# Gated linear attention and a hard-swish feed-forward on one core: keys and queries turned in token pairs, growth products written over alpha, another order of steps

## The chip, the cores and the metric

One NeuronCore of one Trainium2 chip runs the whole kernel as one launch. The metric is the device time of an execution in microseconds (us). Engines are named as in the profile: PE (TensorE, matmuls), PEld (its weight loads), DVE (VectorE), ACT (ScalarE), POOL (GpSimd) and SP (the queue that issues all DMAs here).

## The reference

Cut to what matters; all tensors are float32 in their values, and the two weight matrices arrive as float64.

```python
# q, k, v, alpha: (B=4, H=8, S=768, D=48)
state = zeros(B, H, D, D)
for t in range(S):
    state = alpha[:, :, t, :, None] * state + einsum('bhd,bhe->bhde', k[:, :, t], v[:, :, t])
    y[:, :, t] = einsum('bhd,bhde->bhe', q[:, :, t], state)
x = y.transpose(0, 2, 1, 3).reshape(3072, 384)
h = x @ w_in                       # (384, 2048)
out = (h * clip(h + 3, 0, 6) / 6) @ w_out   # (2048, 384)
```

## The kernel before, in words

**Chunks.** The recurrence is computed in 24 chunks of 128 tokens, six per batch entry, all eight heads at once as four pairs of heads. A chunk needs keys, queries and alpha with head and feature on the partitions and tokens along the free axis. For chunk j these steps exist, named by the words of the order described below:

- `la`, `lk`, `lq`, `lv`: loads of alpha, keys, queries, values (DMAs on SP, L251 to L272). `ta`, `tk`, `tq`: the turn to feature-major. For chunks 0 to 5 PE does it (L282); from chunk 6 on (`FIRST = 6`) the loads are laid out so that VectorE's 32x32 block transpose does it (L286), writing straight into the tile of the keys or queries, every fourth word in a row. `ca` puts alpha into `aX[j % 2]` (L300 on ScalarE, or L286).
- `r` (`decay`): a scan backwards over alpha gives R (L309), and a reciprocal fills the first column of `ini[j % 2]` (L313). `p` (`growth`): a scan forwards over alpha, started by `ini`, gives P (L320). `k` and `q` (`scaled`): keys times R, queries times P, in place (L332).
- `sc` (L346) is the scores, `m` (L356) the mask, `qa` (L366) places queries for the part of the state, `kb` and `ck` (L374, L378), or `kt`, `kw`, `kr` (a block transpose on VectorE at L391, then out to DRAM and back), bring keys to token-major. `u` (L430) is the update of the state, `sm` (L440) and `st` (L409, POOL) carry the state on, `sv` (L419, ScalarE) puts it beside the values. `ya` and `yb` (L456) are attention over the two halves of the chunk, `cy` (L465) copies the result out as x.

The matmuls of `sc`, `u`, `ya` and `yb` are small: 48x64, 64x48 and 128x32 tiles of the array, 32 records to a step (16 for a `u` with one bank). Everything else on PE uses the whole array. A run of consecutive small steps is called a block below.

**Feed-forward.** Two chunks make a group g of 256 tokens, twelve groups. Groups 0 and 1 multiply by w_in plainly (`f`, `fa`, `fb`: L479, L490). From group 2 on a scheme of 20 products is used: `xc` adds up inputs (VectorE, 128x128), `M` is a product (L603, eight records), `n` (L609, ScalarE) keeps partial sums, `o` (L540 to L544, VectorE) adds up outputs, `e` and `h` (L495 on ScalarE, L499 on VectorE) are the activation. The second matmul is plain for group 0 (`b`, L517); from group 1 on it has seven products `P` (L706, 16 records), with sums `s` (L650, L667), `K` and `G` (copies and sums of outputs) and stores `O`. `w`, `d1` to `d4`, `x`, `y` load and convert the weights early in the run. PE is thus asked for the same matmuls whatever the order.

**The order.** One string of 1798 words, written out in the code, sets the program order of all engines (`with tc.manual_schedule(): run("...")`, from L757 on). A word is a step with its chunk or group and, behind further dots, its part and the PSUM bank that it takes: `sc.9.0.1` is the scores of chunk 9 in banks 0 and 1. Each engine issues its own instructions in this order and waits on semaphores for the others. DMAs stand in the same order on SP's queue. POOL has little in it: conversion of weights early (L217), then `st` and four clears of values (L415).

Of the kernel before, what the change touches and what calls it, by code (L numbers as in the profile page):

```python
# [8 lines left out]
FP = mybir.dt.float32  # L9
# [8 lines left out]
def kernel(  # L18
# [86 lines left out]
    aX, ini = [], []  # L105
    for r in range(2):
        t = consts.tile([C, NP * W + 1], FP, tag=f"ax{r}")
        nc.vector.memset(t, 0.0)
        aX.append(t)
        t = consts.tile([C, NP * W], FP, tag=f"ini{r}")  # L110
        nc.vector.memset(t, 0.0)
        ini.append(t)
# [114 lines left out]
    Ps = consts.tile([C, NP * W], FP, tag="P", name="P")  # L227
# [46 lines left out]
    def transposed(name, j, i=None):  # L274
        if j >= FIRST:
            t = (K_t if name == "k" else Q_t)[j] = (Ks if name == "k" else Qs)[j % 2]
            by_blocks(t, name, j)
            return
        t = bank("t" + name, j, i)
        src = ring[name, j % NR]  # L280
        for p in range(NP):
            nc.tensor.transpose(  # L282
                t[:, p], src[:, 2 * p : 2 * p + 2].rearrange("s h d -> s (h d)"), ident)

    def by_blocks(to, name, j):
        nc.vector.transpose(out=to.rearrange("r p (u v) -> r p v u", v=V),  # L286
                            in_=quads[name, j % NQ][:, :, :, 0:BLK])

# [5 lines left out]
    def without_first(t):  # L294
        return t[:, 0 : NP * W].rearrange("r (p w) -> r p w", w=W)[:, :, 1:W]
# [8 lines left out]
    def decay(j):  # L304

        n = NP * W
        ax, ic = aX[j % 2], ini[j % 2]
# [5 lines left out]
        nc.vector.reciprocal(out=ic.rearrange("r (p w) -> r p w", w=W)[:, :, 0:1],  # L313
                             in_=R_t[j][:, :, 0:1])

    def growth(j):

        n = NP * W
        P_t[j] = Ps
        nc.vector.tensor_tensor_scan(  # L320
            out=P_t[j], data0=aX[j % 2][:, 0:n], data1=ini[j % 2], initial=0.0,
            op0=ALU.mult, op1=ALU.add)

    def scaled(name, j):

        if j < FIRST:
            src = ps_t.pop(("t" + name, j))
            t = (Ks if name == "k" else Qs)[j % 2]
        else:
            src = t = (K_t if name == "k" else Q_t)[j]  # L330
        by = R_t[j][:, :, 1:W] if name == "k" else without_first(P_t.pop(j))
        nc.vector.tensor_tensor(out=t, in0=src, in1=by, op=ALU.mult)  # L332
        (K_t if name == "k" else Q_t)[j] = t
# [423 lines left out]
    with tc.manual_schedule():  # L757
# [14 lines left out]
               d2.8 cy.3 d3.8 fr.0.6.1 w.9 ca.6 w.4 fr.0.7.0 fg.0.7 lv.4.1 ck.4 d2.9 d3.9 f.1.1.1  # L772
               q.4 st.4 d1.9 fr.1.1.0 fg.1.1 sv.4.0 f.1.0.2 ca.5 sc.4.1.0 u.4.1.0 fg.0.6 r.5 d1.4
               f.1.7.0 r.6 f.1.3.3 d4.8 d2.4 w.10 tk.5.3 d4.9 w.11 dx.4 fr.1.7.1 sm.4.0 d3.4 w.12
               d2.10 qa.4.0 fg.1.7 fr.1.3.1 m.4 lq.5 d1.10 f.1.6.0 d3.10 d1.12 d4.4 fr.1.0.0 f.1.2.1
               p.5 fg.1.3 d2.12 k.5 fg.1.0 d3.12 d4.10 fr.1.6.1 sm.4.1 tq.5.1 sv.4.1 lk.6 w.13
               fr.1.2.0 d1.11 f.1.4.2 d2.11 d4.12 fg.1.6 q.5 d3.11 p.6 d2.13 la.7 fr.1.4.1 fg.1.4
               f.1.5.0 lv.5.0 qa.4.1 fg.1.2 kb.5.3 fr.1.5.1 w.15 d4.11 d2.15 ca.7 ya.4.1 qa.5.1 tk.6
               yb.4 sc.5.2.0 b.1.0.2 lk.7 k.6 d3.13 d3.15 st.5 ck.5 fa.4.3 m.5 b.1.1 lq.6 w.14 tq.6
               fb.4 fg.1.5 d1.13 d1.15 d4.15 q.6 b.0.0.1 d2.14 fr.0.4.0 d3.14 y.5 d4.13 cy.4 fg.0.4  # L780
               d1.14 d4.14 x.0 y.1 y.10 b.0.1 y.0 y.2 u.5.2 P.1.0.0 K.1.0 qa.5.0 sv.5.0 qa.6.1
               P.1.1.3 b.0.2 b.1.2 kb.6.0 ya.5.3 y.6 s.1.0.0 sm.5.0 sv.5.1 G.1.0.0 tk.7 s.1.1.1
               s.1.2.3 x.1 yb.5 cy.5 b.1.3 sc.6.1.2 lv.6.2 ck.6 u.6.3.0 s.1.3.2 x.2 P.1.2 b.0.3
               K.1.1 y.7 s.1.4 s.1.5 y.11 y.3 r.7 xc.2.1 x.3 y.4 y.8 xc.2.3 k.7 xc.2.0 xc.2.4 y.9
               y.12 y.16 y.13 y.15 P.1.3.3 K.1.2 P.1.4 bo.1 P.1.5 xc.2.5 G.1.1.1 P.1.6 y.14 y.17
               la.8 xc.2.2 xc.2.6 y.19 G.1.3.3 so.1 y.20 G.1.2.2 y.18 M.2.0.2 bo.0 y.21 M.2.15.3
               y.23 sm.6.0 n.2.0.8 z.1.3 M.2.1 M.2.16 xc.2.8 n.2.1.9 xc.2.7 M.2.2 kb.7.3 p.7 lk.8
               O.1.2 lq.7 xc.2.10 sm.6.1 n.2.2.10 ca.8 m.6 M.2.7.0 lq.8 n.2.7.11 M.2.3 M.2.4 M.2.8
               xc.2.9 lv.7.0 r.8 n.2.4.12 tk.8 ck.7 lv.12.1 k.8 M.2.18.1 sv.6.1 o.2.0.0 st.7 M.2.5
               tq.7 kt.8 kw.8 n.2.5.13 M.2.9 q.7 o.2.1.0 sv.6.0 lq.9 o.2.4.0 u.7.1.3 sc.7.1.3 sm.7.0  # L790
               sv.7.0 O.1.3 M.2.10 ya.6.2 yb.6 e.2.1.1 la.9 h.2.1 e.2.0.0 y.22 lv.8.2 p.8 n.2.10.14
               qa.7.0 M.2.11 sv.7.1 M.2.6.2 n.2.18.10 M.2.19 h.2.0 n.2.11.15 qa.7.1 m.7 O.1.1 M.2.12
               cy.6 o.2.6.0 o.2.5.0 ya.7.1 yb.7 n.2.12.12 kr.8 xc.3.2 y.24 M.2.13 lv.9.0 o.2.3.0
               n.2.13.12 cy.7 tq.8 lq.10 sm.7.1 o.2.3.1 M.2.17 o.2.2.0 e.2.3.0 M.2.14 o.2.2.1 xc.3.1
               xc.3.3 la.10 e.2.2.1 P.2.0.1 xc.3.4 xc.3.5 lk.10 xc.3.6 M.3.0.2 q.8 u.8.1.0 lk.9
               sc.8.2.3 n.3.0.12 M.3.1 h.2.2 e.2.5.1 h.2.3 xc.3.0 xc.3.7 o.2.6.1 e.2.6.0 M.3.7.0
               n.3.1.9 o.2.7.0 o.2.7.1 K.2.0.3 h.2.6 M.3.2 P.2.1 qa.8.0 n.3.7.13 e.2.4.0 n.3.2.10
               xc.3.10 xc.3.8 st.8 h.2.5 ca.9 M.3.3 O.1.0 qa.8.1 h.2.4 r.9 s.2.0.14 G.2.0.1 e.2.7.0
               h.2.7 s.2.1.11 xc.3.9 M.3.4 n.3.4.8 s.2.2.15 M.3.8 P.2.3.3 o.3.0.0 K.2.2 tk.9
               s.2.3.14 s.2.5 k.9 e.3.0.1 M.3.9 o.3.1.0 M.3.5 kt.9 n.3.5.11 P.2.2 sm.8.0 s.2.4 la.11  # L800
               K.2.1 M.3.10 M.3.18.2 P.2.5 sm.8.1 e.3.1.0 n.3.18.15 tq.9 m.8 M.3.19 n.3.10.14 p.9
               M.3.11 ca.10 h.3.0 sv.8.0 q.9 kw.9 qa.6.0 G.2.2.0 kr.9 n.3.11.8 h.3.1 o.3.6.0 sv.8.1
               qa.9.0 P.2.4 o.3.5.0 sc.9.0.1 u.9.2.3 qa.9.1 M.3.12 r.10 n.3.12.10 M.3.15.2 st.9
               tk.10 m.9 M.3.16 M.3.6.3 sv.9.0 G.2.1.2 M.3.13 sm.9.0 o.3.7.0 O.2.2 ya.8.0 yb.8
               o.3.4.0 o.3.3.0 sv.9.1 k.10 ya.9.2 yb.9 n.3.13.10 cy.8 kt.10 sm.9.1 M.3.14 ca.11 cy.9
               o.3.6.1 e.3.5.0 xc.4.1 h.3.5 O.2.1 xc.4.3 xc.4.4 xc.4.0 xc.4.5 e.3.4.1 M.3.17 xc.4.6
               P.2.6 e.3.6.0 st.10 h.3.4 xc.4.2 xc.4.10 lk.11 kw.10 o.3.2.0 o.3.2.1 M.4.0.0 O.2.0
               G.2.3.3 e.3.2.1 xc.4.7 o.3.3.1 o.3.7.1 n.4.0.10 h.3.2 xc.4.8 P.3.0.1 M.4.1 K.3.0.2
               e.3.3.1 h.3.3 n.4.1.13 tq.10 e.3.7.1 P.3.1 p.10 M.4.2 q.10 kr.10 G.3.0.0 lv.10.2
               M.4.7.3 n.4.2.14 la.12 h.3.6 M.4.3 n.4.7.15 h.3.7 lk.12 s.3.0.9 M.4.4 n.4.4.8  # L810
               s.3.1.11 lv.11.0 M.4.8 r.11 P.3.3.2 sc.10.0.2 sv.10.0 s.3.2.12 o.4.0.0 u.10.1.3 tk.11
               O.2.3 M.4.9 s.3.3.9 P.3.2 p.11 K.3.2 k.11 K.3.1 s.3.5 M.4.5 qa.10.0 kt.11 o.4.1.0
               s.3.4 M.4.10 n.4.10.9 m.10 ca.12 P.3.5 sm.10.0 e.4.0.0 lq.11 n.4.5.11 xc.4.9 r.12
               kw.11 M.4.11 G.3.2.1 h.4.0 tq.11 e.4.1.1 la.13 sm.10.1 tk.12 qa.12.0 sv.10.1 M.4.18.0
               P.3.4 n.4.18.12 q.11 kr.11 sv.12.0 M.4.19 G.3.1.3 o.4.6.0 n.4.11.8 M.4.12 o.4.5.0
               st.11 k.12 qa.10.1 u.11.0 lq.12 h.4.1 qa.11.1 sv.11.0 sm.11.0 tq.12 sc.11.1.2 sv.11.1
               la.14 n.4.12.14 kt.12 P.3.6 M.4.6.2 qa.11.0 o.4.3.0 G.3.3.2 M.4.13 m.11 n.4.13.14
               ca.13 kw.12 ya.11.1 yb.11 cy.11 ya.10.2 o.4.2.0 qa.18.0 o.4.2.1 e.4.2.1 o.4.3.1 yb.10
               M.4.15.1 p.12 cy.10 M.4.16 q.12 xc.5.1 M.4.14 e.4.3.0 xc.5.0 xc.5.3 o.4.4.0 lk.13
               O.3.3 xc.5.4 h.4.3 xc.5.5 kr.12 O.3.1 P.4.0.2 M.5.0.0 o.4.6.1 xc.5.6 e.4.4.0 xc.5.7  # L820
               xc.5.2 M.4.17 h.4.4 lv.13.2 h.4.2 e.4.5.0 n.5.0.14 o.4.7.0 e.4.6.1 u.12.3.0 sc.12.3.0
               o.4.7.1 M.5.1 K.4.0.3 h.4.5 tk.13 h.4.6 s.4.0.11 n.5.1.13 e.4.7.1 r.13 M.5.7.1 lk.14
               lq.13 s.4.2.9 P.4.1 h.4.7 xc.5.8 G.4.0.3 s.4.1.12 p.13 M.5.2 tq.13 n.5.2.15 P.4.3.3
               k.13 M.5.3 M.5.4 lq.14 s.4.3.10 K.4.2 sm.12.0 kt.13 n.5.7.8 sm.12.1 O.3.2 s.4.5
# [116 lines left out]
```

## Time and profile before

| what | value |
|---|---|
| median of 3 runs | 533.34 us (533.32 to 534.0) |
| the profiled execution | 533.63 us, of which the trace's span is 531.8 us |
| granted TensorE clock, whole span | 1.0 |
| HBM | 44.50 MB read, 8.91 MB written |
| DMA queue's share of 16 engines' span | 42.2% |
| last matmul ends | 528.95 us into the span |

The span runs from the first to the last instruction of the trace; 1.8 us lie around it. A line of a group reads: source line, engine, operation, output<-inputs with shapes, count, then busy us and mean ns of one, then the idle time of the engine just ahead of them and what ended it. Two instructions of one engine overlap a little, so their distance from start to start is shorter than a mean duration. Idle time of an engine that is not the bottleneck costs nothing.

### The profile page before, as it was taken

Reading aid. Unit: us, or ns where it says so; the run is one execution under the profiler, and the core shown is the slowest. Engines: PE = TensorE matmul, PEld = TensorE weight load, DVE = VectorE, ACT = ScalarE, POOL = GpSimd, SP = SyncE. Lnnn points to the kernel's source line nnn. Section 1 sums busy time; section 2 is a strip of 40 time slices with the busy share of each in tenths; the row PEclk is TensorE's granted clock in tenths of the full one; section 3 lists DMA queues with packets and bytes.
Section 4 is the critical chain, followed back from the end, with each engine's and each line's share of the span. In section 5 each row is a group of like instructions: output and inputs, shape, how many; then the busy total and the mean of one; then the engine's idle time right before and its main releaser. Section 6 shows DMA issues by size and latency. Waiting matters only on the chain.

```text
span 531.8 us, 15076 instructions
## 1 busy us (share of the span) xinstructions
PE 524.3 (99%) x6290; PEld 494.0 (93%) x6290; DVE 475.6 (89%) x839; ACT 261.4 (49%) x513; POOL 50.3 (9%) x71
## 2 busy tenths in 40 slices
PE   8999999999999999999999999999999999999997
PEld 5798886789999999999999999999999999999997
DVE  7999999999999999999999999998999999486471
ACT  4888875212664453542673554544454454443330
POOL 5333353100000100000000000000000000000000
PEclk9999999999999999999999999999999999999999
DMA  9999867005363253453463553443531532010000
GB/s 177 246 241 251 247 153 177 2 2 133 74 150 84 64 118 77 115 123 89 95 156 85 120 136 91 96 107 69 145 78 20 129 98 48 1 33 7 9 17 30
DMA packets 124100, 54.40 MB, mean 102 GB/s; under 512 B 83328, under 2 KB 116864, under 8 KB 124032
## 3 DMA queue, kind: packets, MB, share of 16 engines
q1 hardware_dynamic: 124032, 53.44, 42.2%
q8 instruction: 49, 0.80, 0.7%
q14 instruction: 19, 0.16, 0.1%
HBM read 44.50 MB, written 8.91 MB: 100 GB/s over the span
## 4 chain that ended last, share of the span: by engine, by line
PE 85%; DVE 7%; ACT 4%; DMA 1%; issue 1%; SPq 1%; POOL 0%; DVEq 0%; ACTq 0%
PE m_ps L706 36%; PE m_ps L603 31%; PE m_ps L479 4%; PE m_ps L517 4%; PE t_ps L456 4%; PE t_ps L346 2%; PE t_ps L430 2%; DMA rings<-in_q_dram 1%; DVE A L356 1%; ACT A L366 1%; DVE g_sb L540 1%; ACT r L495 1%; ACT raw L186 1%; DVE g_sb L499 1%; SPq L251 1%
## 5 line engine op out<-in xcount | busy, mean ns | idle before, releaser
L706 PE MATMUL m_ps<-w,g_sb 128*128 128x192 f32 x704 | 121.7, 326 | 0.0
L609 ACT COPY g_sb<-m_ps 128x512 f32<-128x512 f32 x110 | 63.5, 584 | 104.2 <-PE m_ps L603 86.4
L706 PEld LDWEIGHTS m_ps<-w,g_sb 128*128 128x128 f32 x704 | 113.7, 190 | 0.6 <-DVE g_sb L667 0.3
L706 PE MATMUL m_ps<-rings,g_sb 128*128 128x192 f32 x528 | 91.7, 327 | 0.2 <-DVE g_sb L650 0.2
L706 PEld LDWEIGHTS m_ps<-rings,g_sb 128*128 128x128 f32 x528 | 85.3, 190 | 0.6 <-DVE g_sb L650 0.5
L603 PE MATMUL m_ps<-xc,w 128*128 128x128 f32 x640 | 83.5, 277 | 0.0
L603 PEld LDWEIGHTS m_ps<-xc,w 128*128 128x128 f32 x640 | 77.9, 192 | 1.1
L495 ACT ACTIVATE r<-g_sb,half 128x512 f32<-128x512 f32 x80 | 57.0, 722 | 29.8 <-DVE g_sb L499 11.9
L499 DVE SCALAR_TENSOR_TENSOR g_sb<-r,g_sb 128x512 f32<-128x512 f32 x80 | 53.5, 682 | 8.7 <-ACT r L495 8.4
L603 PE MATMUL m_ps<-xT,raw 128*128 128x128 f32 x400 | 52.8, 277 | 0.0
L603 PEld LDWEIGHTS m_ps<-xT,raw 128*128 128x128 f32 x400 | 48.8, 192 | 0.5 <-ACT g_sb L609 0.2
L409 POOL TENSOR_TENSOR st<-sm,R 128x192 f32<-128x192 f32 x20 | 12.6, 630 | 358.2 <-DVE sm L440 300.5
L650 DVE TENSOR_TENSOR g_sb<-g_sb 128x512 f32<-128x512 f32 (+1 forms) x55 | 42.1, 792 | 3.7 <-PE m_ps L706 3.5
L603 PE MATMUL m_ps<-xT,w 128*128 128x128 f32 x320 | 42.0, 277 | 0.0
L603 PEld LDWEIGHTS m_ps<-xT,w 128*128 128x128 f32 x320 | 39.0, 192 | 0.4
L366 ACT COPY A<-q 48x256 f32<-48x256 f32 x88 | 35.4, 403 | 7.3 <-DVE q L332 6.1
L356 DVE TENSOR_TENSOR A<-t_ps,mask 64x256 f32<-64x256 f32 x96 | 36.2, 416 | 1.2 <-PE t_ps L346 0.8
L479 PE MATMUL m_ps<-xT,w 128*128 128x256 f32 x144 | 33.3, 384 | 0.5 <-POOL w L217 0.3
L603 PE MATMUL m_ps<-xc,raw 128*128 128x128 f32 x240 | 32.1, 277 | 0.1
L479 PEld LDWEIGHTS m_ps<-xT,w 128*128 128x128 f32 x144 | 26.5, 190 | 5.3 <-POOL w L217 0.9
L540 DVE TENSOR_TENSOR g_sb<-g_sb 128x512 f32<-128x512 f32 x40 | 27.2, 682 | 4.6 <-ACT g_sb L609 4.6
L309 DVE TENSOR_TENSOR_SCAN R<-t,ones 128x516 f32<-128x516 f32 x24 | 29.6, 1233 | 1.6 <-ACT t L300 1.6
(105 smaller groups left out, 726.9 us busy)
## 6 DMA issues: line engine op xcount, KB each, us to landing
raw<-in_moe_w_out_dram SPq DMA_DIRECT2D x8, 768.0 KB, 5.5
raw<-in_moe_w_in_dram SPq DMA_DIRECT2D x6, 768.0 KB, 7.3
v<-in_v_dram SPq DMA_DIRECT2D x48, 96.0 KB, 3.1
out_dram<-oh SPq DMA_DIRECT2D x44, 96.0 KB, 1.8
far<-kq SPq DMA_DIRECT2D x64, 64.0 KB, 2.2
kb<-far SPq DMA_DIRECT2D x64, 64.0 KB, 2.0
aq<-in_alpha_dram SPq DMA_DIRECT2D x36, 96.0 KB, 2.5
kq<-in_k_dram SPq DMA_DIRECT2D x36, 96.0 KB, 2.5
```

The costliest lines, as they stand in the source:

```text
L309: nc.vector.tensor_tensor_scan(out=reverse(R, n - 1, n), data0=reverse(ax, n, n), data1=reverse(ones, n, n), initial=0.0, op0=ALU.mult, op ...
L356: nc.vector.tensor_tensor(out=to[:, a], in0=sc[a][half], in1=mask[half, half].unsqueeze(1).to_broadcast([HB, NP, HB]), op=ALU.mult)
L366: nc.scalar.copy(out=to[:, a], in_=Q_t[j][64 * a : 64 * a + D, :, half])
L456: nc.tensor.matmul(y_of(j, (i + 1) // 2, p)[:, HB * b : HB * b + HB], vb[:, p, e : e + 32], A_t[j][:, b, 2 * p + a], start=(b == 0 and i = ...
L479: nc.tensor.matmul(h[:, f], w1[:, kk, o : o + C], xT_t[g][:, kk], start=(kk == 0), stop=(kk == KT - 1))
L495: nc.scalar.activation(out=to, in_=h, func=AF.Relu, bias=half, scale=1.0 / 6.0)
L499: nc.vector.scalar_tensor_tensor(out=to, in0=r, scalar=1.0, in1=h, op0=ALU.min, op1=ALU.mult)
L540: eng.tensor_tensor(out=out, in0=in0, in1=in1, op=ALU.add if s1 > 0 else ALU.subtract)
L603: nc.tensor.matmul(acc[g][i][:, f * C : (f + 1) * C], spots[w][:, f * C : (f + 1) * C], x_of(g, x), start=(first and f == 0), stop=last, s ...
L609: nc.scalar.copy(out=slots[z], in_=acc[g][i])
L650: nc.vector.tensor_tensor(out=out, in0=in0, in1=in1, op=ALU.subtract)
L706: nc.tensor.matmul(to[g], a, rhs[:, f], start=(first and f == 0), stop=(last and f == HF - 1), skip_group_check=True)
```

## The change

Three things.

1. From chunk 6 on the block transpose of keys and queries no longer writes the tile that the matmuls read. It writes a tile `kt` or `qt`, one for each name, in which tokens lie in pairs: every second word in a row. The multiply by R or P reads these pairs and writes the tile of the keys or queries in the order of the tokens. Alpha is turned as before.
2. From chunk 6 on the growth scan writes its products over alpha in `aX[j % 2]`, so the tile P goes; for the chunks ahead of that it writes to `qt`. There is one `ini` in place of two. Since the scan overwrites the zeros in the first column of each pair of heads, a memset of 128x4 words on POOL puts them back after the queries are multiplied, 18 times in all.
3. The words of the order behind the 200th stand in another order, and some take other banks; the last three are the same. The steps are the same ones.

The code, cut to its core:

```diff
-    aX, ini = [], []
+    aX = []
...
-        t = consts.tile([C, NP * W], FP, tag=f"ini{r}")
-        nc.vector.memset(t, 0.0)
-        ini.append(t)
+    ini = consts.tile([C, NP * W], FP, tag="ini")
+    nc.vector.memset(ini, 0.0)
...
-    Ps = consts.tile([C, NP * W], FP, tag="P", name="P")
+    places = {name: consts.tile([C, NP * W], FP, tag=f"{name}t", name=f"{name}t")
+              for name in "kq"}
+    turns = {name: t[:, 0 : NP * C].rearrange("r (w p n) -> r w p n", w=2, p=NP)
+             for name, t in places.items()}
...
     def transposed(name, j, i=None):
         if j >= FIRST:
-            t = (K_t if name == "k" else Q_t)[j] = (Ks if name == "k" else Qs)[j % 2]
-            by_blocks(t, name, j)
+            turned(name, name, j)
             return
...
+    def turned(to, name, j):
+        nc.vector.transpose(
+            out=turns[to].rearrange("r w p (u b) -> r p w b u", b=V // 2),
+            in_=quads[name, j % NQ].rearrange("r p (w b) d -> r p w b d", w=2)[..., 0:BLK])
+
+    def in_pairs(to):
+        return turns[to].rearrange("r w p (u b) -> r p u w b", b=V // 2)
+
+    def pairs(x):
+        return x.rearrange("r p (u w b) -> r p u w b", w=2, b=V // 2)
...
     def growth(j):
-        P_t[j] = Ps
-        nc.vector.tensor_tensor_scan(
-            out=P_t[j], data0=aX[j % 2][:, 0:n], data1=ini[j % 2], initial=0.0,
-            op0=ALU.mult, op1=ALU.add)
+        P_t[j] = places["q"] if j < FIRST else aX[j % 2]
+        to = P_t[j][:, 0:n]
+        nc.vector.tensor_tensor_scan(out=to, data0=aX[j % 2][:, 0:n], data1=ini, initial=0.0,
+                                     op0=ALU.mult, op1=ALU.add)

     def scaled(name, j):
...
+        if j < FIRST:
+            nc.vector.tensor_tensor(out=t, in0=ps_t.pop(("t" + name, j)), in1=by, op=ALU.mult)
+            return
+        nc.vector.tensor_tensor(
+            out=pairs(t), in0=in_pairs(name), in1=pairs(by), op=ALU.mult)
+        if name == "q":
+            first = aX[j % 2][:, 0 : NP * W].rearrange("r (p w) -> r p w", w=W)[:, :, 0:1]
+            nc.gpsimd.memset(first, 0.0)
```

The order, as far as it is spoken of: the blocks of small steps behind the 200th word, in turn, without banks. Before, 31:

```
sc.4 u.4 | ya.4 yb.4 sc.5 | u.5 | ya.5 yb.5 | sc.6 u.6 | u.7 sc.7 | ya.6 yb.6 | ya.7 yb.7 | u.8 sc.8 |
sc.9 u.9 | ya.8 yb.8 ya.9 yb.9 | sc.10 u.10 | u.11 sc.11 | ya.11 yb.11 ya.10 yb.10 | u.12 sc.12 |
u.13 sc.13 | ya.13 ya.12 yb.12 yb.13 | u.14 sc.14 | u.15 sc.15 | ya.15 ya.14 yb.14 yb.15 | sc.16 u.16 |
u.17 sc.17 | u.18 ya.17 yb.17 ya.16 yb.16 | sc.18 sc.19 u.19 | ya.18 ya.19 yb.18 yb.19 | u.20 sc.20 |
u.21 sc.21 | ya.20 yb.20 ya.21 yb.21 | u.22 | u.23 sc.23 sc.22 | ya.22 yb.22 ya.23 yb.23
```

After, 25:

```
u.5 u.4 sc.4 sc.5 | ya.5 yb.5 ya.4 yb.4 | u.7 u.6 sc.6 sc.7 | ya.6 yb.6 | ya.7 yb.7 | sc.8 u.8 |
sc.9 u.9 | ya.8 ya.9 yb.9 yb.8 | sc.10 u.10 | u.11 sc.11 | ya.11 yb.11 ya.10 yb.10 | sc.13 sc.12 u.12 |
u.13 | ya.12 yb.12 ya.13 yb.13 | u.15 u.14 sc.14 sc.15 | ya.15 yb.15 ya.14 yb.14 | u.17 u.16 sc.17 sc.16 |
ya.16 yb.16 ya.17 yb.17 | sc.19 sc.18 u.18 u.19 | ya.19 ya.18 yb.19 yb.18 | u.20 u.21 sc.21 sc.20 |
ya.21 yb.21 ya.20 yb.20 | u.22 | u.23 sc.23 sc.22 | ya.23 yb.23 ya.22 yb.22
```

Three places of the new order that are spoken of, with what stands between left out:

```
... K.7.1 sm.18.0 sm.18.1 q.20 sv.18.1 st.19 sm.19.0 xc.8.9 k.20 ...
... kr.11 n.4.5.11 q.12 u.11.0 sv.11.0 G.3.2.1 sv.10.1 ca.14 ...
... q.11 P.3.2 lk.13 p.12 la.13 k.12 sm.10.1 K.3.1 M.4.10 qa.10.0 h.4.0 ca.13 ...
```

## Prediction

> **What bounds the kernel now.** I read the busy shares and the slices first, then the chain, then PE's own waits, then the stretches, and last single blocks of PE and VectorE.
>
> ```profile
> PE 524.3 (99%) x6290; PEld 494.0 (93%) x6290; DVE 475.6 (89%) x839; ACT 261.4 (49%) x513; POOL 50.3 (9%) x71
> ...
> DVE  7999999999999999999999999998999999486471
> ...
> PE 85%; DVE 7%; ACT 4%; DMA 1%; issue 1%; SPq 1%; POOL 0%; DVEq 0%; ACTq 0%
> ```
>
> Two engines are full at once: PE over the whole span, VectorE in all but the last sixth. Which of them sets the end is told by who waits. PE's waits from 55 us on, complete:
>
> ```profile
> PE m_ps L479 <- DVE g_sb L499: 0.2, 1, 0.2
> PE m_ps L706 <- DVE g_sb L650: 0.2, 1, 0.2
> ```
>
> PE sets it; VectorE follows just in time. But matmul records overlap, so a busy PE hides short stops. I therefore took the starts of the matmuls: a step's usual time is the usual distance from its first matmul to that of the next step, with the same kinds of neighbours (a product M: 0.89 us between large ones, a product P: 2.60). From the first PE step behind the 200th (54.7 us) to the last product's start (526.2) there are 471.5 us. The steps' usual times add up to 468.4. So **3.0 us** are lateness, and I found it at 72 to 76 us (0.7), 127 (0.2), 147 to 156 (1.0), 240 (0.25), 410 (0.45), the rest in crumbs. That, and the 468.4 itself, is all that a new order can win; the 200 steps ahead are the same, and so are the last three.
>
> How near VectorE is, by stretches (length, then busy us of PE, PEld, DVE, ACT, POOL):
>
> ```profile
> 232.00:274.00 42.00, 42.00 (x540) 41.04 (x540) 40.77 (x77) 19.93 (x42) 1.84 (x3) 1.00 0.47 110
> ...
> 434.50:477.00 42.50, 42.50 (x508) 42.05 (x497) 30.22 (x60) 19.77 (x40) 0.51 (x1) 1.00 0.14 37
> ```
>
> A group of two chunks takes 40 to 42 us and VectorE is busy in 97% of it, until the chunks run out.
>
> **Part 1, the turns.** The groups of VectorE that matter (busy us, mean ns):
>
> ```profile
> L286 DVE STREAM_TRANSPOSE k<-kq 128x512 f32<-128x512 f32 x18 | 20.1, 1116 | 0.5 <-PE t_ps L346 0.4
> L332 DVE TENSOR_TENSOR k<-k,R 128x512 f32<-128x512 f32 x18 | 12.3, 685 | 0.1
> ...
> L391 DVE STREAM_TRANSPOSE kq<-k 128x512 f32<-128x512 f32 x16 | 11.2, 698 | 0.1
> ...
> L210 DVE SCALAR_TENSOR_TENSOR raw<-raw,w 128x768 uint32<-128x768 uint32 x11 | 10.6, 960 | 0.4
> ```
>
> L286 writes every fourth word (16 bytes apart) and takes 1116 ns; L391 turns as many elements, writes consecutive words and takes 698. The new turn of keys and queries writes every second word (8 bytes). No turn of the trace does that, so its cost lies between 698 and 1116. L210 reads and writes every second word: 256 elements more than L332 cost 275 ns more, 1.07 ns each, against 685/512 = 1.34 with the fixed part: no penalty at 8 bytes. I take 698. Instructions overlap a little, so what counts is start to next start: 0.96 us for L286, 0.63 for L391, 0.33 saved each; 36 turns (k and q of 18 chunks) are **12 us of VectorE**; alpha's 18 turns stay.
>
> The Trainium skill ("Advanced Engine Details and Errata", SBUF Cachelines) states lines of 16 bytes, of which two accesses in a row must hit one for full speed. By it the new turn, with two hits a line, costs what the contiguous one does, and the sum is the one above; by the upper row nothing would be saved. No run so far shows the form.
>
> The multiply (L332) now reads the turned keys as pairs, two words here and two 1 KB further; out and factor stay in order. It has 685 ns in the trace with everything in order. Nothing shows pairs: from below it is the 685, from above 685 + 418, if it fell to the pace of L286. I take 685, since a pair lies within the same 16 bytes as in L210.
>
> **Part 2, growth over alpha, one `ini`.** The scan L320 keeps its length (1267 ns mean) and writes where it read: 0; the nearest row is L309, a scan of the same length at 1233. One opening memset (0.49 us) goes; it lay under alpha's first load, which lands at 9.4 us. New are 18 memsets of 4 words on POOL: its small memsets (L257) take 145 to 324 ns, so some 3 to 5 us on an engine that is 9% busy. They add a wait: alpha's turn and the scan of two chunks later (VectorE) wait for POOL, and POOL's `st` queues behind a memset that waits for the q multiply. In the new order the q multiply nearly always stands far ahead. The tightest is chunk 19: `sm.18.1 q.20 sv.18.1 st.19 sm.19.0`, where VectorE has nothing between q.20 and sm.19.0: 0.15 (memset) + 0.63 (L409) + the handing over, about 1 us of VectorE. There VectorE is over 15 us ahead of PE by the addition below; without that cover it would be 1 us of the span. I cost it at nothing. Two more handings over (ca.14 behind q.12, ca.13 behind q.11) have 0.3 and 2.6 us of VectorE work between.
>
> **Part 3, the order.** All steps are the same; only banks and places change. PE's work is the same matmuls, but a change between 64-row or 32-column tiles and full ones costs time (start us, us):
>
> ```profile
> 396.27 1.06 PE L603 MATMUL m_ps<-xT,raw 128*128 128x128 f32 x8
> 397.26 0.57 PE L430 MATMUL t_ps<-v,kb 64*48 64x48 f32 x32
> 397.65 0.66 PE L346 MATMUL t_ps<-q,k 48*64 48x64 f32 x32
> 398.24 1.16 PE L603 MATMUL m_ps<-xc,w 128*128 128x128 f32 x8
> 399.24 1.06 PE L603 MATMUL m_ps<-xT,raw 128*128 128x128 f32 x8
> 400.13 0.65 PE L706 MATMUL m_ps<-w,g_sb 128*128 128x192 f32 x3
> ```
>
> Start to start, the last product ahead of the small block takes 0.99, the first behind it 1.00, an undisturbed one 0.89: 0.10 and 0.11 per block. Within, two attentions in one block take less than twice one, by the chain's pieces:
>
> ```profile
> 105.24 1.03 PE t_ps L456 x64
> ...
> 183.50 1.92 PE t_ps L456 x128
> ```
>
> 2 x 1.03 - 1.92 = 0.14. So each block that is merged into another saves 0.21 to 0.35 us. Behind the 200th step the old order has 31 such blocks, the new one 25: 6 x 0.21 = 1.3 to 6 x 0.35 = 2.1. Adding all steps with their neighbours gives 1.7. **I take 1.9.**
>
> Then the lateness. I added VectorE's steps of both orders, each at its start-to-start time. Up to the first product of group 5 the old order has 170.3 us of VectorE behind the 200th step, the new one 175.6: it spends the saving at once on preparing chunks earlier (16 turns done there, not 14). PE gets there at 177.4 now, having waited 2.0. In the old order VectorE was idle 7.9 us up to there (178.2 from its first step to that place, less 170.3), so it has less to spare: set against the PE step that needs it, the smallest lead falls from 2.8 us to 1.4 (P.2.3, about 160 us) and from 5.7 to 2.7 (M.5.9, about 245 us), before any idling. I charge **0.8 us** more lateness ahead of 250 us. Behind that the lead grows to 40 us (old: 30), and most of the 0.9 us of old lateness there should go: **-0.6**. What is late next is PE's own issue.
>
> Sum against the profiled execution, 533.63 us (span 531.8 and 1.8 around it): -1.9 + 0.8 - 0.6 = -1.7, 531.9. The median of the runs is 0.29 lower: **531.6 us**.
>
> **Rivals.** (a) VectorE's lead is too thin: the new order is paced for it ahead of 250 us, and idling like the old order's 7.9 us, half of it kept, would make PE late by 4.0 - 2.7 + 0.5 for handing over, about 1.8: with -1.9 and nothing gained behind, 533.2, no change. For: two full engines in lockstep. Against: an engine that is behind finds its inputs ready and idles less. (b) **Slower:** pairs read (or every second word written) at the pace of L286, 0.33 us more for each of two instructions a chunk. VectorE gets its 12 us back, yet the order has already spent them: up to M.5.9 that is 16 instructions, 5.3 us, on a lead of 2.7, with 0.5 for handing over 3.1 us of lateness, and 1.4 of idling on top (a sixth of the old 7.9): 533.34 - 1.9 + 4.5 = 536. It decides from 0.17 us per instruction (16 x 0.17 - 2.7 + 0.5 + 1.4 = 1.9). For: 16-byte steps do cost that here. Against: L210. That the turns get no faster at all, so the change doesn't do what it says, is this case too, with the same price. (c) Everything falls into place: lateness drops from 3.0 to 1, 533.34 - 1.9 - 2.0 = 529.4.
>
> **How the numbers follow.** Forecast (530.6 to 532.2) 0.45; (c) 0.17; (a) 0.18; (b) 0.20. About 0.2% (1.1 us) is what a measurement of this kernel can tell from no change. Faster by more: forecast and (c), 0.62; within: (a), 0.18; slower: 0.20. The range takes (c), (a) and the lower part of (b), which with its bounds reaches past 536: 529.0 to 535.2.
>
> **What would show it.** Right: the pair turn at about 700 ns and alpha's still at 1116; the pair multiply at 685; VectorE's busy sum near 463 us (475.6 - 12 - 0.5); 25 blocks of small tiles; PE's starts from the 200th step to the last product within 470.5 us. Wrong: a pair multiply over 800 ns; PE waits for VectorE (L603 or L706) between 130 and 250 us; ScalarE or VectorE waiting long for POOL.

## The result, and the profile after

The kernel after takes **539.99 us** in the median of 5 runs (538.65 to 540.93), the kernel before 533.34 (532.74 to 534.0) on the same chip: a ratio of 1.012, 95% interval 1.010 to 1.014. The forecast was 531.6, and its range (529.0 to 535.2) does not hold the time. The profiled execution, the longest of the five, took 540.93 us, its span 539.1.

Line numbers shift: the turn L286 is L291 for keys and queries and L287 for alpha, the multiply L332 is L343, the products L603 and L706 are L617 and L720, the activation L499 is L513.

From the page of the kernel after: busy shares, VectorE's slices, the chain.

```profile
PE 525.0 (97%) x6290; PEld 495.0 (92%) x6290; DVE 463.9 (86%) x838; ACT 260.6 (48%) x513; POOL 53.1 (10%) x89
...
DVE  6999988999999999999899988589988899386381
...
PE 50%; DVE 32%; SPq 6%; DMA 6%; issue 4%; ACT 1%; DVEq 0%; POOL 0%; ACTq 0%
```

VectorE has 11.7 us less to do, and yet its part of the chain that ended last rose from 7% to 32%. SP's queue and DMAs, 2% together before, have 12%. So PE now stops and waits. The list of PE's waits behind 55 us had two lines of 0.2 us; in the kernel after it is this (who waits and for which line, us in total, times, longest):

```profile
PE m_ps L720 <- DVE g_sb L513: 1.6, 1, 1.6
PE m_ps L617 <- DVE g_sb L554: 1.1, 3, 0.7
PE t_ps L444 <- DMA kb<-far: 0.9, 2, 0.7
PE m_ps L617 <- issue: 0.8, 1, 0.8
PE t_ps L360 <- DVE sm L454: 0.8, 1, 0.8
PE m_ps L720 <- DVE rings L664: 0.7, 1, 0.7
PE t_ps L360 <- DVE s L452: 0.5, 1, 0.5
PE m_ps L617 <- DVE g_sb L558: 0.5, 1, 0.5
PE m_ps L493 <- DVE g_sb L513: 0.5, 1, 0.5
PE m_ps L617 <- DVE oh L740: 0.2, 1, 0.2
```

No line is large. The prediction's own addition (each step's usual time from start to start, behind the 200th step) splits the time: the usual times fell from 468.4 to 466.7, and the lateness on top of them rose from 3.1 to **12.7 us**. Where it lies, by what the trace names at each place (a time in brackets is the start of the step ahead of the late one):

| lateness in the kernel after | us |
|---|---|
| ScalarE late behind a weight's DMA: P.1.0 (84 us), and f.1.4.2 (70 us) | 1.7 + 0.6 |
| one VectorE step far back in VectorE's order: P.1.2 (110 us); inputs of the first M.2 and M.2.9 (120 to 138 us) | 0.8 + 1.2 |
| a wait inside a merged block: sc.7 (131 us), sc.15 (288 us) | 0.7 + 1.0 |
| SP's queue, in which a write had waited for VectorE's turn of keys: u.8 (156 us), u.12 (238 us) | 1.0 + 0.5 |
| VectorE behind: 221 to 236 us, M.5.9 (252), 332, M.8.15 (396) | 0.9 + 0.9 + 0.3 + 0.6 |
| "issue", always within M.5.14 (272 us) | 0.9 |
| crumbs | 1.6 |

Three of these places as the timeline of the kernel after shows them (start us, us, engine, line, tiles, and in brackets the idle time ahead and what ended it). First M.5.9, with the growth scan and alpha's turn of a later chunk in front of the output sum (L554) that it needs:

```profile
250.32 1.23 DVE L333 TENSOR_TENSOR_SCAN t<-t,ini 128x516 f32<-128x516 f32 x1
251.46 1.09 DVE L287 STREAM_TRANSPOSE t<-aq 128x512 f32<-128x512 f32 x1
...
252.58 0.69 DVE L554 TENSOR_TENSOR g_sb<-m_ps,g_sb 128x512 f32<-128x512 f32 x1
...
253.32 0.94 PE L617 MATMUL m_ps<-xc,w 128*128 128x128 f32 x6 [0.70 <-DVE g_sb L554]
```

Then the merged block `u.7 u.6 sc.6 sc.7`: the second scores can't start until VectorE has copied an update out of the bank, which stands behind other work there.

```profile
130.87 0.66 PE L360 MATMUL t_ps<-q,k 48*64 48x64 f32 x32
...
131.62 0.35 DVE L452 COPY s<-t_ps 128x192 f32<-128x192 f32 x1
...
132.03 0.69 PE L360 MATMUL t_ps<-q,k 48*64 48x64 f32 x32 [0.49 <-DVE s L452]
```

And SP's queue ahead of `u.8`, which needs the keys that come back from DRAM (`kb<-far`). Each DMA takes SP 0.4 to 0.9 us to issue, in order:

```profile
142.72 3.43 SPq L410 DMA_DIRECT2D far<-kq  x4
146.19 2.05 SPq L264 DMA_DIRECT2D kq<-in_k_dram  x4
...
150.24 2.04 SPq L264 DMA_DIRECT2D qq<-in_q_dram  x4
152.32 2.67 SPq L418 DMA_DIRECT2D kb<-far  x4
```

```profile
156.82 0.38 PE L444 MATMUL t_ps<-v,kb 64*48 64x48 f32 x14 [0.71 <-DMA kb<-far]
```

The read `kr.8` stands two words ahead of `u.8` in the new order (28 before), behind fifteen other issues since 142.7 us; a transfer of this kind lands 2.0 us after its issue in the page's median. Four of the fifteen are the write of the same keys, which the read has to follow; for it SP had waited 7.9 us, by its own list of waits, until VectorE had turned them (L405, done at 142.7). The other eleven took 6.1 us. At `u.12` the read stands behind the write of chunk 13's keys, and that waits from 225.1 to 231.7 us for VectorE's turn, with chunk 12's write already issued.

### The profile page after: what moved, and what is told of

Read it like the earlier page. It is cut to its first block, busy times and chain, and to the rows that moved or that the text cites. A ratio compares the mean times of both kernels' runs of the same rounds, so it can differ in the third digit from the quotient of the medians.

```text
span 539.1 us, 15090 instructions
## 1 busy us (share of the span) xinstructions
PE 525.0 (97%) x6290; PEld 495.0 (92%) x6290; DVE 463.9 (86%) x838; ACT 260.6 (48%) x513; POOL 53.1 (10%) x89
## 4 chain that ended last, share of the span: by engine, by line
PE 50%; DVE 32%; SPq 6%; DMA 6%; issue 4%; ACT 1%; DVEq 0%; POOL 0%; ACTq 0%
PE m_ps L720 23%; PE m_ps L617 23%; DVE A L370 4%; DVE g_sb L513 3%; DMA raw<-in_moe_w_out_dram 3%; SPq L264 2%; DVE R L321 2%; PE t_ps L470 2%; DVE g_sb L554 2%; SPq L418 1%; DMA rings<-in_q_dram 1%; DVE raw L209 1%; DVE t L333 1%; DVE t L287 1%; DVE g_sb L664 1%
## 5 line engine op out<-in xcount | busy, mean ns | idle before, releaser
L720 PE MATMUL m_ps<-w,g_sb 128*128 128x192 f32 x704 | 121.8, 326 | 1.7 <-DVE g_sb L513 1.6
L720 PEld LDWEIGHTS m_ps<-w,g_sb 128*128 128x128 f32 x704 | 113.8, 190 | 3.1 <-DVE g_sb L513 2.2
L720 PE MATMUL m_ps<-rings,g_sb 128*128 128x192 f32 x528 | 91.7, 327 | 0.7 <-DVE rings L664 0.7
L720 PEld LDWEIGHTS m_ps<-rings,g_sb 128*128 128x128 f32 x528 | 85.2, 190 | 1.5 <-ACT p L699 0.9
L617 PE MATMUL m_ps<-xc,w 128*128 128x128 f32 x640 | 84.0, 277 | 1.9 <-DVE g_sb L554 0.9
L509 ACT ACTIVATE r<-g_sb,half 128x512 f32<-128x512 f32 x80 | 56.6, 721 | 51.9 <-DVE g_sb L558 22.1
L617 PEld LDWEIGHTS m_ps<-xc,w 128*128 128x128 f32 x640 | 78.1, 192 | 3.7 <-DVE g_sb L554 1.6
L513 DVE SCALAR_TENSOR_TENSOR g_sb<-r,g_sb 128x512 f32<-128x512 f32 x80 | 54.1, 687 | 12.9 <-ACT r L509 12.5
L617 PE MATMUL m_ps<-xT,raw 128*128 128x128 f32 x400 | 52.9, 277 | 0.5 <-DVE g_sb L558 0.5
L617 PEld LDWEIGHTS m_ps<-xT,raw 128*128 128x128 f32 x400 | 48.7, 192 | 1.3 <-DVE g_sb L558 0.6
L617 PE MATMUL m_ps<-xT,w 128*128 128x128 f32 x320 | 41.9, 276 | 0.0
L617 PEld LDWEIGHTS m_ps<-xT,w 128*128 128x128 f32 x320 | 39.3, 192 | 0.5
L554 DVE TENSOR_TENSOR g_sb<-g_sb 128x512 f32<-128x512 f32 x40 | 27.0, 681 | 12.1 <-ACT g_sb L623 12.1
L617 PE MATMUL m_ps<-xc,raw 128*128 128x128 f32 x240 | 32.1, 277 | 0.2 <-DVE g_sb L554 0.2
L617 PEld LDWEIGHTS m_ps<-xc,raw 128*128 128x128 f32 x240 | 29.6, 192 | 0.9 <-DVE g_sb L554 0.5
```

The costliest lines, as they stand in the source:

```text
L509: nc.scalar.activation(out=to, in_=h, func=AF.Relu, bias=half, scale=1.0 / 6.0)
L513: nc.vector.scalar_tensor_tensor(out=to, in0=r, scalar=1.0, in1=h, op0=ALU.min, op1=ALU.mult)
L554: eng.tensor_tensor(out=out, in0=in0, in1=in1, op=ALU.add if s1 > 0 else ALU.subtract)
L617: nc.tensor.matmul(acc[g][i][:, f * C : (f + 1) * C], spots[w][:, f * C : (f + 1) * C], x_of(g, x), start=(first and f == 0), stop=last, s ...
L720: nc.tensor.matmul(to[g], a, rhs[:, f], start=(first and f == 0), stop=(last and f == HF - 1), skip_group_check=True)
```

## Experiments

My theory (O) was that the code is good and the new order is what costs, by VectorE's thin lead and by single places; the rivals, that the code itself costs (C), and, within O, which of the two kinds of cause it is. All ratios are to the kernel before, on the same chip, with 95% intervals; "usual" and "lateness" are the two parts named above, from the profiled execution. The rows come from several chips, on which the median of the kernel before was 533.31 to 533.54.

| kernel | median us | ratio | usual | lateness |
|---|---|---|---|---|
| before | 533.34 | | 468.4 | 3.1 |
| after | 539.99 | 1.010 to 1.014 | 466.7 | 12.7 |
| e1_old_order | 535.76 | 1.003 to 1.006 | 468.4 | 5.8 |
| e11_old_order_r6_three_later | 533.22 | 0.999 to 1.001 | 468.4 | 3.0 |
| e5_old_order_p5_first | **532.68** | 0.9978 to 0.9995 | 468.4 | 2.4 |
| e6_old_order_by_fours | 534.29 | 1.001 to 1.003 | 468.4 | 4.4 |
| e4_turn_by_fours | 546.57 | 1.023 to 1.026 | 466.7 | 17.3 |
| e2_new_then_old | 535.1 | 1.002 to 1.004 | 467.5 | 4.3 |
| e3_old_then_new | 546.55 | 1.022 to 1.028 | 467.6 | 18.3 |
| e8_after_no_scan | 537.67 | 1.007 to 1.010 | 466.7 | 8.3 |
| e7_after_mended | 537.66 | 1.007 to 1.012 | 467.3 | 8.7 |
| e9_after_mended_more | 535.9 | 1.004 to 1.006 | 467.3 | 5.9 |
| e10_mended_more_no_scan | 532.74 | 0.998 to 1.000 | 467.3 | 3.1 |

### Code and order apart: e1, e11, e5

The code of the kernel after runs in the order of before if three scans or multiplies are moved, since there is one `ini` and one `kt`. In e1:

```diff
 (order of before, code of after)
-... r.5 d1.4 f.1.7.0 r.6 ... p.5 fg.1.3 d2.12 k.5 fg.1.0 ...
+... r.5 d1.4 f.1.7.0 ... p.5 r.6 fg.1.3 d2.12 k.5 fg.1.0 ...
```

> The changed code (pair turn, growth over alpha, one ini, memsets on POOL) with the order of before; only three words of it are moved, because one ini and one place for keys ask for it (r.6 behind p.5, p.17 ahead of r.18, k.21 ahead of tk.22). Theory O (the new order makes PE late; the code is sound): VectorE has 12 us less to do, PE has the 31 blocks of before, lateness at most the 3.0 us of before: 531.5 to 533.5 us. Rival C (growth over alpha, its waits for POOL or the pair multiply make engines late): near 540 us, with VectorE waiting for POOL.

Measured 535.76, above before, which by itself would speak for C. But 4.1 of its 5.8 us of lateness lie between 71 and 76 us, right behind the moved step. The timeline of e1 shows the scan of 1.22 us taking twice that, beside a conversion on POOL; first POOL, then VectorE:

```profile
68.64 2.27 POOL L216 TENSOR_TENSOR w<-raw 128x768 int32<-128x768 int32 x1 [3.11 <-ACT raw L185]
```

```profile
69.57 2.43 DVE L321 TENSOR_TENSOR_SCAN R<-t,ones 128x516 f32<-128x516 f32 x1
```

The scan ends 1.1 us after the conversion does: it ran, in effect, once POOL was done. So I took the collision away, in two ways. e5 moves `p.5` ahead of `r.6` instead:

```diff
-... r.5 d1.4 f.1.7.0 ... p.5 r.6 fg.1.3 ...
+... r.5 p.5 d1.4 f.1.7.0 r.6 ... fg.1.3 ...
```

> The code after, steps in the order of before; of the steps that the one tile of reciprocals forces to move, this time the forward scan p.5 goes ahead of r.6 (behind r.5) and r.6 stays where it was before, so that no scan falls beside the conversion of POOL that doubled one in e1_old_order; p.17 ahead of r.18 and k.21 ahead of tk.22 as there. Theory O (the code is good, the order is what costs): 4.1 us of e1's lateness were r.6's new place, so 535.8 - 4.1 = 531.7, and up to 0.8 more for p.5's 1.2 us ahead of L449: 531.5 to 532.5, below the kernel before. Theory C (the code costs something by itself, by the memsets, the division's tile or the pair reads): 533.3 or more.

Measured 532.68: 3.1 below e1, and **0.65 below the kernel before** (0.9978 to 0.9995). It is 0.2 above what O expected at most, but on O's side of before. e11 leaves the scan in the stage where e1 had put it, three VectorE instructions later:

```diff
-... p.5 r.6 fg.1.3 d2.12 k.5 fg.1.0 d3.12 ...
+... p.5 fg.1.3 d2.12 k.5 fg.1.0 r.6 d3.12 ...
```

> e1_old_order with one step moved: the backward scan r.6 stands behind fg.1.0 instead of directly behind p.5, three VectorE instructions (L513, L341, L513) later and still ahead of L206, so that it starts when POOL's conversion of a weight (L216, 68.6 to 70.9 us in e1) is over. If the overlap with POOL is what cost e1 3.1 us against e5_old_order_p5_first, the scan takes 1.22 instead of 2.43 us and the time falls to 532.7 to 533.3. If the place is what cost (a scan among activations that PE waits for), the scan still delays what is behind it by 1.2 us and the time falls by 1.2 at most: 534.5.

Measured 533.22, 2.5 below e1. In its timeline the scan stands alone and has its usual length:

```profile
71.60 1.23 DVE L321 TENSOR_TENSOR_SCAN R<-t,ones 128x516 f32<-128x516 f32 x1
```

So the move took away 2.5 of e1's 3.1 us, more than the 1.2 that the place alone could give. It changed two things at once: by the two lengths, 2.43 and 1.23 us, an estimate is that about half of the 2.5 is the overlap with POOL, and the other half that the scan no longer stands ahead of two activations. The Trainium skill ("SBUF — State Buffer", SBUF: two separate sides) states that a VectorE instruction with two SBUF inputs and a GpSimd instruction that reads SBUF lock each other out for the whole instruction. The trace agrees: 2.43 us is 1.3 us of waiting for the conversion's end and 1.2 of scan, nearly. Theory C falls: in e5 the code alone makes the kernel a little faster, and in e11 it changes nothing that can be told from before.

### What the fast turn is worth: e4, e6

Both turn keys and queries into the same places with 16-byte steps, as before, and multiply whole tiles.

```diff
-            out=turns[to].rearrange("r w p (u b) -> r p w b u", b=V // 2),
-            in_=quads[name, j % NQ].rearrange("r p (w b) d -> r p w b d", w=2)[..., 0:BLK])
+        by_blocks(flat(to), name, j)
...
-            out=pairs(t), in0=in_pairs(name), in1=pairs(by), op=ALU.mult)
+            out=t, in0=flat(name), in1=by, op=ALU.mult)
```

> The changed code and order, but keys and queries are turned with a step of four words, as before the change, into the same two places, and multiplied without pairs. Each of the 36 turns goes back from 705 to about 1115 ns. Theory O: the new order has spent VectorE's 12 us ahead of 250 us, where VectorE already makes PE late; up to there 16 turns at 0.33 come back as PE lateness: 540 + 5, 543 to 547 us. Rival (VectorE's work isn't what makes PE late in the new order, but DMAs and ScalarE): 540 to 541.

> The same order as e5_old_order_p5_first, with the turn of 16-byte steps into the same places (36 turns at 1.11 instead of 0.70 us, the multiply on whole tiles). In the new order the fast turn was worth 6.6 us (e4_turn_by_fours against after). Theory O: the old order has slack on VectorE wherever it needs it, so the fast turn is worth little there: 0.3 to 1.5 us above e5. Rival (VectorE's 12 us count in any order alike): about 6.6 us above e5, 538.

In the new order the fast turn is worth 546.57 - 539.99 = 6.6 us, as theory O expected; in the old one 534.29 - 532.68 = 1.6, a little more than expected, and far from the rival's 6.6. The same 12 us of VectorE are worth four times as much in the new order, so it leaves VectorE much less lead. That e6 is 0.95 above before, with turns as slow, suggests that the rest of the change (the single `ini`, growth over alpha, the moved steps) costs something; I did not take that apart.

### Halves of the order: e2, e3

e2 takes the new order to its 545th word (about 155 us) and finishes in the old one; e3 takes the old one to its 548th word and finishes in the new one (both with e1's move of `r.6` where it applies).

> The changed code; the new order for its first 545 words (to about 155 us), then what is left in the old order (same three repairs). In the trace of after, PE is 7.1 us late between 60 and 155 us (before: 2.0) and 5.6 behind that (before: 1.1). Theory O, with each stretch late by itself: 533.3 + 5.1 for the first stretch, less 2 merged blocks at 0.3, 537 to 538.5 us. Rival O2 (VectorE's early spending makes the later stretch late as well, whatever its order): 540 or more. Rival C: near 540.

> The changed code; the old order for its first 548 words (to about 155 us, r.6 behind p.5), then what is left in the new order. Theory O, each stretch late by itself: 533.3 + 4.5 for the second stretch, less about 3 merged blocks at 0.3, 536 to 538 us. Rival O2 (the second stretch is late only because the first left VectorE behind): 531 to 533. Rival C: near 540.

e2, 535.1, lies 2 us below what O expected. Its waits at 120 to 156 us are those of the kernel after (sc.7 0.68, M.3.1 1.03), with 0.2 behind, so O2 falls: the new first stretch doesn't make the old second one late. P.1.2 is in time here; why is open. The wait at 84 us did not come. It hangs on when a weight lands: between 74 and 90 us ScalarE waits 5.9 us for weights in the kernel after, 4.9 in e8, 3.0 in e4 and 1.7 in e2, all with the same steps there. e3, 546.55, is far above O's 538 and above all its own: 4.1 us are e1's collision and 7.2 arise at the seam (160 to 175 us). But from 240 to 300 us it has the places of the kernel after one by one: M.4.17 0.4, M.5.9 0.8, the issue 0.9, sc.15 1.0. So they come behind the old first stretch as well; since e3 lost time ahead of them too, it doesn't show whether a start without losses would spare them.

### Single places, or VectorE altogether: e8, e7, e9, e10

e8 takes work off VectorE, in the same order:

```diff
-        nc.vector.tensor_tensor_scan(out=to, data0=aX[j % 2][:, 0:n], data1=ini, initial=0.0,
-                                     op0=ALU.mult, op1=ALU.add)
+        if j < FIRST:
+            nc.vector.tensor_tensor_scan(out=to, data0=aX[j % 2][:, 0:n], data1=ini, initial=0.0,
+                                         op0=ALU.mult, op1=ALU.add)
```

> The kernel after, with the growth products of chunks 6 on left out: the queries are multiplied by alpha itself, so 18 scans of 1.215 us (21.9 us of VectorE) are gone and the order is the same. Theory V (VectorE is what the new order waits for): lateness falls from 12.7 to the part that names DMA, bank and ScalarE, about 5 us, so 531 to 533. Theory L (single waits of the order, whoever is named): those with DMA, banks and ScalarE stay and some of VectorE's too, 536 or more.

Measured 537.67, only 2.3 below the kernel after: theory V (VectorE is what it waits for) is refuted in its plain form, by a kernel that has 21.9 us less on VectorE. What went are the places at 221 to 252 us and at 396, u.12 among them, and most of sc.7; what stayed are P.1.2 (0.8), M.3.1 (0.9), sc.15 (1.0) and the issue (0.9), and half of the wait behind the weight (0.9). e7 mends five places and leaves the work:

```diff
-... d2.13 fr.0.4.0 ... d1.15 fr.1.5.1 ...
+... fr.0.4.0 d2.13 ... fr.1.5.1 d1.15 ...
-... sc.7.3.0 sm.6.1 bo.0 st.7 M.2.2 ...
+... sm.6.1 bo.0 st.7 M.2.2 sc.7.3.0 ...
-... sc.15.3.0 m.15 k.16 M.6.3 ...
+... k.16 M.6.3 sc.15.3.0 m.15 ...
 (kw.8, kr.8, kw.12, kr.12: 14 to 36 words earlier)
```

> The kernel after with five places of its order mended: d2.13 and d1.15 behind the activations of group 1; sc.7 one matrix step later; sc.15 and m.15 behind M.6.3; the write and the read of chunk 8's keys through DRAM (kw.8, kr.8) 19 to 36 words earlier, those of chunk 12 some 14 to 28 words earlier. If the lateness is a list of single waits (theory L): -0.5 (sc.7), -0.9 (sc.15), -1.0 (M.3.1), -0.4 (M.4.17), and up to -1.7 where the weight load is late, together 536.5 to 537.5, and those five lines vanish from the trace. If VectorE is too late all through the stretch (theory V), the same time is waited for at the next step that needs VectorE: 539 to 540.

Measured 537.66, 2.3 below the kernel after, theory L's side but a little short. Four of the five places are gone from its timeline (M.2.9, which comes next behind sc.7's old place, now waits 0.7 us, 0.4 more). The fifth is not: `u.8` still waited, 0.9 us. The list of waits names a load of queries there, but that was issued later; the values of chunk 8 (`lv.8.2`), which `u.8` reads, were issued at 149 us, 3 us ahead of it, behind five groups of other transfers, and a load of values takes 3.1 us to land. So I took them for the cause. e9 moves them too, and two places of VectorE:

```diff
-... la.10 ... lv.8.2 ...
+... lv.8.2 la.10 ...
-... x.1 y.5 s.1.5 sv.5.1 G.1.0.0 y.7 k.7 y.8 x.2 ...
+... x.1 x.2 y.5 s.1.5 sv.5.1 G.1.0.0 y.7 k.7 y.8 ...
-... P.4.3.3 p.14 ... M.5.9 ...
+... P.4.3.3 ... M.5.9 p.14 ...
```

> The order of e7_after_mended with three more places mended: the values of chunk 8 (lv.8.2) loaded ahead of chunk 10's alpha and chunk 9's keys, since in e7 the wait at M.3.1 stayed (1.2 us) and SyncE issued those values, behind eight other transfers, 3 us before they were used; the difference x.2 directly behind x.1, in front of y.5 to y.8 and k.7; the growth scan p.14 behind M.5.9 instead of behind P.4.3. Theory L (single waits of the order): 1.2 at M.3.1, 0.7 at P.1.2 and 1.1 at M.5.9 go, so 537.7 - 3.0 = 534.7; with the M.5.9 wait only moved on to the next user of VectorE, 535.7. Theory V (VectorE is too late all through): 537 or more.

Measured 535.9, beside the 535.7 expected if a wait only moves on. The wait at `u.8` is gone. The two others became smaller or changed places: 1.1 us at M.5.9 became 0.6 at M.5.10, and 0.7 at P.1.2 became 0.9 at P.1.3, while 0.8 us at 117 to 124 us went. PE's waits in e9, all but one for VectorE:

```profile
PE m_ps L617 <- DVE g_sb L558: 0.9, 2, 0.5
PE m_ps L617 <- DVE g_sb L554: 0.8, 2, 0.5
PE m_ps L720 <- DVE oh L740: 0.7, 1, 0.7
PE m_ps L617 <- issue: 0.3, 1, 0.3
```

e10 is e9's order without the scans:

> The order of e9_after_mended_more, with the 18 scans over alpha of chunks 6 on left out as in e8_after_no_scan (the queries are multiplied by alpha itself): 21.9 us less on VectorE. If the lateness of the kernel after is the sum of single places (DMA issue order, banks, ScalarE, one step's place on VectorE) and of a VectorE lead that is too thin behind 220 us, then what is left here is about 3 us of lateness on 467.3 of usual work, 532.5 to 533.5, and 1 to 2 us below e9. If the two kinds of cause are the same one, e10 equals e9 within 0.5.

Measured 532.74, within the range expected, and 3.2 below e9 where 1 to 2 was expected. PE's waits in e10 (lines are one further down):

```profile
PE t_ps L445 <- DMA kb<-far: 0.8, 1, 0.8
PE m_ps L618 <- issue: 0.7, 1, 0.7
```

VectorE is gone from the list. So the 12.7 us were both: single places, of which mending eight took 12.7 - 5.9 = 6.8 us out of the profile (4.1 out of the median: the profiled execution is the longest of five in the kernel after, the shortest of five in e9), and a lead of VectorE that is too thin, for which e10 shows 2.8 more. The two are not one cause, since sc.15 and M.3.1 stay without the scans and go when they are mended. But they overlap: without the scans sc.7, u.12 and, in e10, P.1.3 are mostly gone as well, so some of the single places were late only because VectorE came late to them.

What stays open is the "issue" within M.5.14: PE runs one or two matmuls of it and stops, 0.3 to 0.8 us, in each of after, e7, e8, e9 and e10, and no semaphore in the profile ends the stop. The traces do show one thing there: in each of the five a transfer of 16 KB of the kind "instruction" (queue q8 in the page) starts 2.6 to 2.9 us before PE goes on, and ends 1.2 to 1.5 us before; just ahead of the stop PE runs 128 small matmuls, each with its weight load, in 2 us. That PE had run out of instructions would fit; I tried nothing against it, so this isn't shown.

## Why the prediction was wrong

**The turns: right.** 704 and 706 ns where I took 698; the multiply on pairs 677 and 684 where I took 685; alpha's turn as before. Groups of the kernel after (busy us, mean ns):

```profile
L291 DVE STREAM_TRANSPOSE kt<-kq 128x512 f32<-128x512 f32 x18 | 12.7, 704 | 0.0
L343 DVE TENSOR_TENSOR q<-qt,t 128x512 f32<-128x512 f32 x18 | 12.3, 684 | 1.6 <-ACT A L380 1.6
L287 DVE STREAM_TRANSPOSE t<-aq 128x512 f32<-128x512 f32 x18 | 19.9, 1113 | 0.0
L333 DVE TENSOR_TENSOR_SCAN t<-t,ini 128x516 f32<-128x516 f32 x18 | 21.9, 1215 | 0.1
```

By the Trainium skill's rule of two hits in a 16-byte line ("Advanced Engine Details and Errata", SBUF Cachelines) the trace agrees: writes 8 bytes apart run at the contiguous pace, writes 16 bytes apart take 1113 ns. VectorE's busy sum is 463.9, against "near 463".

**Growth over alpha, one `ini`: right in its parts.** The scan over alpha takes 1215 ns; the 18 memsets are 106 ns each, and no wait for one of them shows. e5 says the code altogether is worth 0.65 us in the old order.

**Fewer blocks: right.** 1.9 us forecast; by the steps' usual times it is 468.4 - 466.7 = 1.7, which is what the addition had said.

**Lateness: the step that failed.** "I charge **0.8 us** more lateness ahead of 250 us", and "-0.6" behind it: together +0.2. It was +9.6 in the profiled execution (12.7 - 3.1): 6.0 ahead of 250 us, and 3.6 behind, with M.5.9 at 252 among it. Two things were wrong with it.

First, I had added the steps of one engine. The addition asked whether VectorE has done enough work by a given time, and by that answer PE could hardly be late. It did not ask whether the other queues have. SP's queue, ScalarE behind a weight, the banks within a merged block, and single VectorE steps placed behind others that nobody waits for yet were in none of the sums, and they are about half of the table above. I had written that every merged block "saves 0.21 to 0.35 us" and not looked at what its second half needs: two of the merged blocks gave back 0.7 and 1.0.

Second, the VectorE lead itself. One of its two places was right: M.5.9, with a lead of 2.7 us "before any idling", is late by 0.9; P.2.3, with only 1.4, is not late at all. By the gaps between its instructions VectorE idled 8.3 us between 60 and 260 us, against 4.7 before; 4.8 of it lies between 60 and 100 us, where two waits for the activation's first half on ScalarE (L509) make 4.1. The extra 3.6 us is more than the lead, but it is not the whole cause: in e9 VectorE idles 4.7 us in the same stretch, as before the change, and PE still waits for it at P.1.3 (0.9) and M.5.10 (0.6). So the leads that the addition gave were too large at these places. One sign of that is in the kernel before: the addition left 7.9 us of idling up to the first product of group 5, where the gaps between VectorE's instructions make 4.5 (55 to 232 us). I did not take this apart further. That "most of the 0.9 us of old lateness there should go" behind 250 us did not hold either: M.8.15 and sc.15 alone are 1.6.

**The rivals.** (a), a lead that is too thin, had the mechanism of the last rows and its place, but priced it at 1.8 us and knew nothing of the queues. (b) gave a time on the right side of no change for a reason that the trace refutes: nothing runs at 1116 ns but alpha. What "would show it wrong" came: between 130 and 250 us PE's L617 waits 0.6 us for VectorE, and sc.7 another 0.5; and PE's starts from the 200th step to the last product take 466.7 + 12.7 = 479.4 us, not "within 470.5".

## What to carry to other kernels

Where an order is set by hand, a sum over one engine only says what can't be late; go down every in-order queue, the DMA issuing one too, and for each step on the critical engine ask what stands ahead of its input there. A change of code that comes with a change of order is best timed with each alone: here the code gains 0.65 us, the order loses 7.3, and the code's saving (6.6 us in one order, 1.6 in the other) can't be priced without the order. Merging small pieces of work saves the switch between them only if what the later pieces need, banks included, is free when the first one ends.

## What the runs showed of the hardware

A scan on VectorE that starts under a POOL conversion takes 2.43 instead of 1.22 us, and moving it by three instructions gave back 2.5 us of a 533 us kernel, by length and place together. The kernels before and after have such scans too (2.28 us at 50 us before, 1.98 us at 65 us after), each beside a conversion. No such stretch came from the 18 memsets. Issuing a DMA holds SP's queue for 0.4 to 0.9 us in the list above: the fifteen issues in front of the one that was needed, four of them its own write, took 9.6 us of the queue, with the DMA engines 29% busy (125 to 160 us).
